# A fused attention and two-FFN kernel: the last matrix of batches 0 and 1 by half products, block sums in place, and a planner with other costs

## The chip, the cores and the metric

The kernel runs on one core of a Trainium2 chip. The metric is the device time of one execution in microseconds, from the first to the last instruction and what lies around them. The time before is the median of three runs.

## The reference

Shapes: q, k, v are (4 batches, 12 heads, 448 positions, 64), so there are 4 x 448 = 1792 tokens of width 768.

```python
scores = q @ k.T / sqrt(64)
scores = cap * tanh(scores / cap)            # cap = 30
attn = softmax(scores)                       # exp, then divided by sum + 1e-9
x = (attn @ v), heads side by side           # 1792 x 768
h = x @ w_in                                 # 768 x 2048
g = where(h >= 1, h, where(h <= -1, 0, (h + 1)**2 / 4))
y = g @ w_out                                # 2048 x 768
m = maximum(maximum(y @ w1, y @ w2), y @ w3) # each 768 x 768
out = m @ w_out2                             # 768 x 768, "the last matrix"
```

The weights arrive as 64-bit floats and are turned into 32-bit ones on the chip.

## The kernel before, in words

Everything is kept transposed: a tile holds 128 features by 448 positions of one batch (two batches side by side in a tile of the pool "u", 35 slots). Precision comes from splitting: a number is held as a rounded high part and the rest, and one **part**, 128 features times a 128 x 448 block, is three matmuls (high x high, high x low, low x high; lines 899 to 901 and 1117). Splitting costs one copy (`copy`, lines 310 and 312, on ScalarE or VectorE) and one subtraction (`tt`, line 315, VectorE).

The order of work is made by `Plan` (line 23). The kernel's functions register steps with `op(cost, fn, want, deps, uses, takes)`: a cost in microseconds for each engine that may do the step (A is ScalarE, D VectorE, T TensorE, Q the DMA queue of SyncE, P GpSimd, S a mere delay without an instruction), the wished time `want`, the steps it depends on and the buffers it takes. `Plan.run` plays the program through with these costs and gives each step to the engine that would end it first; buffers of a pool are handed out in order of `want`. `emit` then writes the instructions in that order, and on the chip each engine works through its own list in order, waiting on semaphores.

In order of time the work is:

- `attention(b, i, ...)` for batch b and pair of heads i (6 pairs): scores, tanh, exp, the sum over keys, the product with v, the division. The sums are made by adding the four key blocks of exp on VectorE (`add` in `attention`, line 717) and then one or more products with ones (`total4`, line 702, `SUM` each). `ADDED = (3, 2, 2, 3)` is the number of additions for each batch: 3 leave one tile for TensorE to sum, 2 leave two tiles. The row of sums is spread over partitions by GpSimd's and SyncE's DMAs (lines 788, 791, 796) around a reciprocal (line 809), and the delays S stand for those DMAs.
- `ffn(0)` for batch 0 while attention of batch 1 runs, then `ffn(1)` while attention of batches 2 and 3 runs. 16 blocks of w_in, 24 blocks of w_out. For batch 0 the weights come as 64-bit words and are made 32-bit in four steps (`fetch_first`, lines 412 to 441), then stored to scratch. The first `PLAIN = 6` blocks of w_in in batch 0 aren't split: `parts` multiplies them by one 32-bit matmul (line 894) with the unsplit `xf`.
- From then on pairs of batches go together, by **half products** (`strassen`, line 1018): a matrix is cut into 2 x 2 blocks and the two batches are the two columns of the other side, and seven products of halves (`STAGES`, line 1016) take the place of eight, at the price of additions. The inputs' sums and their splits (`divide`, t1 to t4, lines 1048 to 1090) fill 7 x K2 tiles named op of pool "u", each held until the last group of outputs has used it; a `lander` (line 1350) adds up the seven results of a group in VectorE and ScalarE. `first_two_end` does this for batches 0 and 1 with the three maximum matrices (layer 2, 9 groups of one block pair), and then takes the last matrix whole: M is split into 12 halves m, and for each of 6 blocks of the weights and each batch 6 parts are summed (lines 1454 to 1482). `last_two` does all four layers for batches 2 and 3 by half products.
- The weight blocks' sums for half products are made by `combine` (line 516: four loads into four wf buffers, four sums into one or two raw buffers), used by `store_sums` and `old_blocks` for batches 2 and 3, and by `new_blocks` (line 1169: sums in two raw buffers) for batches 0 and 1. Pools: raw 3, wf 5, w 4 slots.

Of the kernel before, what the change touches and what calls it, by code (L numbers as in the profile page):

```python
# [22 lines left out]
class Plan:  # L23
# [3 lines left out]

    LATENCY = 0.08  # L30
    AHEAD = 25.0
    TURN = 0.1
    STAY = 5.0
# [39 lines left out]
    def run(self):  # L73
# [42 lines left out]
        while left:  # L116
            moved = True
            while moved:
                moved = False
                ts = [o for o in ready if o.kind and at[id(o)] <= t + 1e-9 and can_take(o)]  # L120
                turn = min(ts, key=first) if ts else None

                only = dict.fromkeys(free_at, 0.0)
                for o in ready:
                    if len(o.cost) == 1 and at[id(o)] <= t + 1e-9:
                        e = next(iter(o.cost))
                        only[e] += o.cost[e]
                for o in ready:
                    if at[id(o)] > t + 1e-9 or o.kind and o is not turn:
                        continue  # L130
                    idle = [e for e in o.cost if free_at[e] <= t + 1e-9]
                    if not idle:
                        continue
                    e = next(iter(o.cost))
                    if len(o.cost) > 1:
                        ends = {e: max(free_at[e], t) + only[e] + c for e, c in o.cost.items()}
                        e = min(ends, key=ends.get)
                    if e not in idle or not can_take(o):
                        continue
# [24 lines left out]
                    left -= 1  # L164
                    moved = True
                    break
# [5 lines left out]
            while events and events[0][0] <= t + 1e-9:  # L172
# [7 lines left out]
                for x in o.out:  # L180
                    x.n -= 1
                    if not x.n:
                        r = max(
                            d.t1 + (0.0 if d.e in x.cost and len(x.cost) == 1 else self.LATENCY)
                            for d in x.deps
                        )
                        if "Q" in x.cost and x.takes:
                            r = max(r, x.want - self.AHEAD)
                        at[id(x)] = r
                        ready.append(x)  # L190
                        serial += 1
                        heapq.heappush(events, (r, serial, None))
# [52 lines left out]
def softcap_attention_two_ffn(  # L245
# [19 lines left out]
    D = 64  # L265
# [55 lines left out]
    def c_tt(n):  # L321
        return {"D": 1.03 * n + 0.155}
# [192 lines left out]
    halves = {}  # L515
    def combine(layer, m, run, want):

        n = RUN[layer]  # L520
        bufs, gots = {}, {}
        for i, j in ((1, 0), (1, 1), (0, 0), (0, 1)):
            u, o = corner(layer, m, i, j, run)
            wf = buf("wf", "wf", [P, WU])

            def load(e, u=u, o=o, wf=wf):
                nc.sync.dma_start(out=wf.tile[:, :n], in_=scratch[u][:, o : o + n])

            bufs[i, j] = wf
            gots[i, j] = op({"Q": 1.7 * n / 1000}, load, want - 8, [stored[u]], takes=[wf])  # L530
        wide = n * 4 * 4 > WU * 8
        ss = [buf("raw", "ss", [P, 2 if wide else 4, n]) for _ in range(2 if wide else 1)]
        c, d = ss[0], ss[-1]

        def s(x):
            return ss[x // 2].tile[:, x % 2] if wide else c.tile[:, x]

        def add(x, y, z, o, deps, uses, takes):
            def get(v):
                return bufs[v].tile[:, :n] if isinstance(v, tuple) else s(v)  # L540

            return op(
                c_tt(n / 1000), lambda e: tt(e, get(x), get(y), get(z), o), want, deps,
                [*uses, *takes], takes,
            )

        s1 = add(0, (1, 0), (1, 1), ALU.add, [gots[1, 0], gots[1, 1]],
                 [bufs[1, 0], bufs[1, 1]], [c])
        s2 = add(1, 0, (0, 0), ALU.subtract, [s1, gots[0, 0]], [bufs[0, 0], c], [])
        s3 = add(2, (0, 0), (1, 0), ALU.subtract, [gots[0, 0], gots[1, 0], s1],  # L550
                 [bufs[0, 0], bufs[1, 0], d], [d] if wide else [])
        s4 = add(3, (0, 1), 1, ALU.subtract, [s2, s3, gots[0, 1]], [bufs[0, 1], c, d], [])
        return s, ss, (s1, s2, s3, s4)

    def store_sums(layer, m, run, want):
        n = RUN[layer]
# [10 lines left out]
    def attention(b, i, begin, last):  # L567
# [207 lines left out]
        if small:  # L775
# [37 lines left out]
            recips.append(  # L813
                op({"Q": 0.7}, spread2, w + 0.3, [r], [rs], [rs] if pooled else [])
            )
        for k in range(0 if small else NCH):
            sl_ = slice(k * C, (k + 1) * C)
            recips.append(op(
# [350 lines left out]
    def new_blocks(layer, group, starts):  # L1169
# [17 lines left out]
            for i in range(2) for j in range(2)  # L1187
        }
        (u1, wf1, g1), (u2, wf2, g2) = wfs
        ss = [buf("raw", "ss", [P, 2 * n]) for _ in range(2)]  # L1190

        def part(x, y):
            return lambda: ss[x].tile[:, y * n : (y + 1) * n]

        s2, s3, s1, s4 = part(0, 0), part(0, 1), part(1, 0), part(1, 1)
        w = starts[2] - 11
# [4 lines left out]
                [*uses, *takes], takes,  # L1201
            )

        o1 = add(s1, a[1, 0], a[1, 1], ALU.add, [g2], [wf2], [ss[1]])
        o2 = add(s2, s1, a[0, 0], ALU.subtract, [o1, g1], [wf1, ss[1]], [ss[0]])
        o3 = add(s3, a[0, 0], a[1, 0], ALU.subtract, [g1, g2, o2], [wf1, wf2, ss[0]])
        o4 = add(s4, a[0, 1], s2, ALU.subtract, [o2, g1], [wf1, *ss])

        def both(get, n, srcs, deps, w):
# [8 lines left out]
            )  # L1218
            return wt, [hi, lo]

        def whole(b_):
            return lambda: b_.tile[:, : 2 * n]

        wa, da = both(whole(wf1), 2 * n, [wf1], [g1], starts[0] - 8)
        keep_divided(u1, wa, da, starts[0])
        wb, db = both(whole(ss[0]), 2 * n, [ss[0]], [o2, o3], starts[2] - 7)
        wc, dc = both(whole(ss[1]), 2 * n, [ss[1]], [o1, o4], starts[4] - 7)
# [211 lines left out]
    def first_two_end(base):  # L1439
# [15 lines left out]
        for j in range(2):  # L1455
            for m in range(NM):
                ms[m][j] = split(
                    "m", lambda m=m, j=j: M[m].tile[:, j], M[m], [mdone[m][j]], base - 4 + 0.1 * m
                )
        for m in range(NM):  # L1460
            u = W2 + m
            wf, got = fetch_again(u, base)
            w = divided(u, wf, got, base)
            if m < H2:
                keep_divided(u, *w, base)
            else:
                keep_divided(u, *w, base, KH)
            for j in range(2):
                ps, g = buf("m", "ps_m", [P, 512]), Group(NP)
                done = parts(  # L1470
                    0, lambda q: base + q * PART, (*w, False), [x[j] for x in ms], 0, NP, ps, g,
                    True,
                )
                for o in done[1:]:
                    o.deps.append(done[0])
                base += NP * PART
                o = half("o")
                c = op(
                    {"A": 0.53, "D": 0.62}, lambda e, o=o, ps=ps: copy(e, o.tile, ps.tile[:, :S]),
                    base, done, [ps], [o],  # L1480
                )
                send(lambda o=o: o.tile, o, m, j, [c], base + 0.6)
        return base

    def last_two(base):
# [127 lines left out]
```

## Time and profile before

| what | value |
| --- | --- |
| median of 3 runs | 955.91 us (955.85 to 959.21) |
| the profiled execution | 959.17 us |
| its span | 957.4 us |
| mean granted TensorE clock | 0.996 of full |
| busy: PE, PEld, DVE, ACT | 98%, 79%, 81%, 62% |
| chain that ended last | PE 90%, DMA 3%, DVE 3%, issue 2%, ACT 1% |

PE is TensorE's matmuls, PEld its weight loads, DVE VectorE, ACT ScalarE, POOL GpSimd, SP SyncE. The windows give the busy time of each engine in a stretch, with instructions in brackets, and then the granted clock, the mean busy share of the DMA engines and GB/s. Busy time counts overlapping instructions once. The chain of waits goes back from the last instruction to what released it each time.

### The profile page before, as it was taken

What the parts mean: (1) busy time and instruction counts of PE and PEld (TensorE: products, weight loads), DVE (VectorE), ACT (ScalarE), POOL (GpSimd) and SP (SyncE); (2) the same over time, 40 slices, a digit from 0 to 9 for tenths busy, and PEclk for the clock granted to TensorE, in tenths of its full rate; (3) what the DMA queues carried; (4) which work ended last, traced back from release to release, by engine and by line L of the source; (5) the groups of instructions that cost most, each with busy time, mean ns of one, the idle gap of its engine ahead of it and who ended that gap; (6) DMA issues with size and microseconds to landing.
All of it is one profiled execution on the core that took longest, in us unless ns stands there. A gap on an engine that the chain in (4) does not pass through costs nothing.

```text
span 957.4 us, 14768 instructions
## 1 busy us (share of the span) xinstructions
PE 937.2 (98%) x5323; PEld 755.6 (79%) x5323; DVE 778.0 (81%) x1288; ACT 594.5 (62%) x932; POOL 14.7 (2%) x27
## 2 busy tenths in 40 slices
PE   7789999999999999999999999999999999999997
PEld 1134788777767676678999999999999999899997
DVE  2898898897989888888888848887889869758782
ACT  7968888775888877774434316566865715233441
POOL 0000000000000000000000000000000000000000
PEclk9989999999999999999999999999999999999999
DMA  7758768998888998853777887442233345446343
GB/s 201 220 154 267 236 191 245 274 287 270 291 280 279 302 292 259 232 173 118 253 265 271 288 295 255 123 140 80 90 101 109 111 121 184 144 147 205 108 148 120
DMA packets 95339, 194.48 MB, mean 203 GB/s; under 512 B 12094, under 2 KB 56858, under 8 KB 95258
## 3 DMA queue, kind: packets, MB, share of 16 engines
q1 hardware_dynamic: 94378, 193.36, 64.0%
q8 instruction: 44, 0.72, 0.3%
q0 software_dynamic: 736, 0.10, 0.1%
q14 instruction: 37, 0.30, 0.1%
q10 hardware_dynamic: 144, 0.00, 0.0%
HBM read 142.51 MB, written 50.81 MB: 202 GB/s over the span
## 4 chain that ended last, share of the span: by engine, by line
PE 90%; DMA 3%; DVE 3%; issue 2%; ACT 1%; SPq 0%; POOL 0%; DVEq 0%; ACTq 0%; POOLq 0%
PE ps_m L1117 32%; PE ps_s L1117 11%; PE ps_m L899 9%; PE ps_m L901 8%; PE ps_m L900 8%; PE ps_a L836 6%; PE ps_s L615 5%; PE ps_a L1117 5%; PE ps_m L894 3%; PE ps_r L709 1%; DMA qk<-in_qk 1%; DMA rc<-rs 1%; DVE op L315 1%; DVE se L315 1%; PE ps_s L626 1%
## 5 line engine op out<-in xcount | busy, mean ns | idle before, releaser
L1117 PE MATMUL ps_m<-op,w 128*128 128x448 f32 x1575 | 324.0, 365 | 0.6 <-DVE M L315 0.6
L1117 PEld LDWEIGHTS ps_m<-op,w 128*128 128x128 f32 x1575 | 295.7, 188 | 24.4 <-DVE M L315 1.0
L315 DVE TENSOR_TENSOR w<-wf,w 128x512 fp32r<-128x512 f32 (+2 forms) x155 | 117.6, 761 | 13.8 <-ACT w L310 11.4
L310 ACT ACTIVATE w<-wf 128x512 fp32r<-128x512 f32 (+2 forms) x120 | 81.1, 679 | 70.4 <-PE ps_m L1117 30.9
L633 ACT ACTIVATE t<-ps_s,qscale 112x896 f32<-112x896 f32 x96 | 93.4, 1004 | 33.0 <-PE ps_s L615 25.2
L1117 PE MATMUL ps_s<-op,w 128*128 128x448 f32 x522 | 110.7, 366 | 0.4 <-DVE op L315 0.2
L1117 PEld LDWEIGHTS ps_s<-op,w 128*128 128x128 f32 x522 | 98.0, 188 | 8.7 <-ACT op L310 0.5
L680 ACT ACTIVATE t<-t,cap_sb 112x896 f32<-112x896 f32 x96 | 95.9, 1038 | 0.3
L310 ACT ACTIVATE w<-ss 128x384 fp32r<-128x384 f32 (+1 forms) x93 | 53.1, 583 | 64.9 <-PE ps_m L1117 37.5
L836 PE MATMUL ps_a<-t,v 112*32 112x448 f32 (+1 forms) x752 | 79.4, 543 | 5.2 <-ACT t L680 2.7
L899 PE MATMUL ps_m<-g,w 128*128 128x448 f32 x192 | 72.6, 378 | 0.0
L315 DVE TENSOR_TENSOR w<-ss,w 128x384 fp32r<-128x384 f32 (+1 forms) x98 | 59.8, 627 | 14.3 <-ACT w L310 14.0
L901 PE MATMUL ps_m<-g,w 128*128 128x448 f32 x192 | 70.3, 366 | 0.0
L900 PE MATMUL ps_m<-g,w 128*128 128x448 f32 x192 | 70.3, 366 | 0.0
L836 PEld LDWEIGHTS ps_a<-t,v 112*32 112x32 f32 (+1 forms) x752 | 22.2, 110 | 51.3 <-issue 33.1
L899 PE MATMUL ps_m<-x,w 128*128 128x448 f32 x156 | 58.7, 376 | 0.0
L423 DVE SCALAR_TENSOR_TENSOR raw<-raw 128x768 int32<-128x768 int32 (+1 forms) x64 | 55.4, 867 | 3.0 <-ACT raw L412 2.5
L900 PE MATMUL ps_m<-x,w 128*128 128x448 f32 x156 | 57.1, 366 | 0.6 <-DVE x L315 0.6
L439 DVE SCALAR_TENSOR_TENSOR wf<-raw 128x768 int32<-128x768 int32 (+1 forms) x64 | 54.7, 856 | 3.1 <-ACT raw L431 1.6
L901 PE MATMUL ps_m<-x,w 128*128 128x448 f32 x156 | 57.0, 366 | 0.0
L1117 PE MATMUL ps_a<-op,w 128*128 128x448 f32 x234 | 51.3, 365 | 0.0
L1117 PEld LDWEIGHTS ps_a<-op,w 128*128 128x128 f32 x234 | 44.0, 188 | 3.5
(142 smaller groups left out, 1424.8 us busy)
## 6 DMA issues: line engine op xcount, KB each, us to landing
wf<-w SPq DMA_DIRECT2D x104, 192.0 KB
wf<-w SPq DMA_DIRECT2D x66, 256.0 KB
w<-wf SPq DMA_DIRECT2D x40, 384.0 KB
wf<-w SPq DMA_DIRECT2D x40, 384.0 KB
raw<-in_w SPq DMA_DIRECT2D x18, 768.0 KB
w<-p SPq DMA_DIRECT2D x36, 384.0 KB
raw<-in_w_in SPq DMA_DIRECT2D x16, 768.0 KB
raw<-in_w_out SPq DMA_DIRECT2D x24, 512.0 KB
```

The source lines that it names most:

```text
L310: nc.scalar.activation(out=out_, in_=in_, func=AF.Copy)
L315: nc.vector.tensor_tensor(out=out_, in0=a, in1=b, op=o)
L423: nc.vector.scalar_tensor_tensor(out=lo, in0=hi, scalar=-(2**31), in1=lo, op0=ALU.bitwise_and, op1=ALU.bitwise_or,)
L439: nc.vector.scalar_tensor_tensor(out=wf.tile[:, :n].bitcast(I32), in0=hi, scalar=3, in1=lo, op0=ALU.logical_shift_left, op1=ALU.bitwise_or,)
L615: nc.tensor.matmul(ps.tile[:C, j, :S], k.tile[o, 1, c * C : (c + 1) * C], q.tile[o, 0], start=n == 0, stop=n == 2,)
L633: nc.scalar.activation(out=t[c].tile, in_=ps.tile[:C, :, :S], func=AF.Tanh, scale=qscale[:C])
L680: lambda e, c=c: nc.scalar.activation(out=t[c].tile, in_=t[c].tile, func=AF.Exp, scale=cap_sb[:C]),
L836: nc.tensor.matmul(pa.tile[j * D + d : j * D + d + n, :S], vt.tile[:, j, c, d : d + n], t[c].tile[:, j], start=start, stop=stop,)
L899: nc.tensor.matmul(ps.tile[:, :S], wh, a.tile[:, 0], start=start, stop=False)
L900: nc.tensor.matmul(ps.tile[:, :S], wh, a.tile[:, 1], start=False, stop=False)
L901: nc.tensor.matmul(ps.tile[:, :S], wl, a.tile[:, 0], start=False, stop=stop)
L1117: nc.tensor.matmul(get(), w_, x_, start=start and z == 0, stop=stop and z == 2, skip_group_check=begun,)
```

## The change

Six edits in one: `first_two_end` hands the last matrix to `strassen` as `last_two` does; `PLAIN` becomes 0; `ADDED` becomes 3 for batches 1 and 2 too; `combine` loads its four blocks by one step into one raw buffer (with a wf buffer for w_out's wider blocks), neighbours in one DMA, and adds in place; `new_blocks` puts its four sums in one raw buffer; the planner's numbers change. Of the last: `LATENCY` 0.09, a `LAP` by which A and D are free again before a step's end, the latency now also between two steps of A or D that follow each other, a delay of 5.0 for batch 0's gather of sums (3.0 before), and a delay of 2.0 behind the spreading DMAs.

```diff
-    LATENCY = 0.08
+    LATENCY = 0.09
+    LAP = {"A": 0.1, "D": 0.08}
...
-                        free_at[e] = t + c
+                        free_at[e] = t + c - self.LAP.get(e, 0.0)
...
-                            d.t1 + (0.0 if d.e in x.cost and len(x.cost) == 1 else self.LATENCY)
+                            d.t1 + (0.0 if d.e == "T" and "T" in x.cost else self.LATENCY)
...
-    PLAIN = 6
+    PLAIN = 0
...
-    ADDED, FOURS, POOLED = (3, 2, 2, 3), (0, 1, 2, 3), ()
+    ADDED, FOURS, POOLED = (3, 3, 3, 3), (0, 1, 2, 3), ()
...
     def combine(layer, m, run, want):
         n = RUN[layer]
-        for i, j in ((1, 0), (1, 1), (0, 0), (0, 1)):
-            u, o = corner(layer, m, i, j, run)
-            wf = buf("wf", "wf", [P, WU])
...
-            gots[i, j] = op({"Q": 1.7 * n / 1000}, load, want - 8, [stored[u]], takes=[wf])
+        fit = 4 * n <= WU * 2
+        raw = buf("raw", "ss", [P, 2 * WU])
+        wf = None if fit else buf("wf", "wf", [P, WU])
...
+                if fit and u == u1 and o1 == o + n:
+                    y = 2 * (1 - i) * n
+                    nc.sync.dma_start(
+                        out=raw.tile[:, y : y + 2 * n], in_=scratch[u][:, o : o + 2 * n]
+                    )
+                    continue
...
+        s1 = add((1, 1), (1, 0), (1, 1), ALU.add, [got])
+        s3 = add((1, 0), (0, 0), (1, 0), ALU.subtract, [s1])
+        s2 = add((0, 0), (1, 1), (0, 0), ALU.subtract, [s1, s3])
+        s4 = add((0, 1), (0, 1), (0, 0), ALU.subtract, [s2])
...
-            r = op({"S": 3.0 if first else 5.0}, lambda e: None, w + 0.06, [r], [rc, src])
+            r = op({"S": 5.0}, lambda e: None, w + 0.06, [r], [rc, src])
...
+            r = op({"Q": 0.7}, spread2, w + 0.3, [r], [rs], [rs] if pooled else [])
+            recips.append(op({"S": 2.0}, lambda e: None, w + 0.3, [r], [rs]))
...
-        ss = [buf("raw", "ss", [P, 2 * n]) for _ in range(2)]
+        ss = [buf("raw", "ss", [P, 2 * WU])]
...
     def first_two_end(base):
...
-        ms = [[None] * 2 for _ in range(NM)]
...
-        for m in range(NM):
-            u = W2 + m
-            wf, got = fetch_again(u, base)
-            w = divided(u, wf, got, base)
...
+        O = [unit(f"O01_{m}") for m in range(NM)]
+
+        def land_o(m, g, i):
+            def finish(i, j, o, w):
+                f = m + H2 * i
+                send(lambda: O[f].tile[:, j], O[f], f, j, [o], w)
+
+            return lander(O[m], O[m + H2], 1, finish)
+
+        base = strassen(
+            3, base, True, list(zip(M, mdone)), [[x] for x in range(N2[3])], land_o, new_blocks,
+            two_banks,
+        )
         return base
```

## Rows read from the trace of the kernel before

**Rows 1.** The page: busy time and instructions of each engine
```profile
PE 937.2 (98%) x5323; PEld 755.6 (79%) x5323; DVE 778.0 (81%) x1288; ACT 594.5 (62%) x932; POOL 14.7 (2%) x27
```
**Rows 2.** Windows (engines PE, PEld, DVE, ACT, POOL): start, two slices with idle PE, end
```profile
0.00:63.50 63.50, 50.63 (x424) 13.28 (x424) 41.59 (x62) 49.55 (x54) 3.36 (x9) 0.96 0.68 192
...
240.00:264.00 24.00, 22.87 (x166) 16.62 (x164) 21.70 (x33) 20.51 (x29) 0.61 (x1) 1.00 0.90 296
...
792.00:816.00 24.00, 23.65 (x116) 21.33 (x115) 21.59 (x42) 15.06 (x31) 0.00 (x0) 1.00 0.53 164
...
952.00:957.40 5.40, 0.23 (x2) 0.00 (x0) 0.00 (x0) 0.55 (x1) 0.00 (x0) 0.93 0.24 84
```
**Rows 3.** Windows: the two FFN stretches, the last matrix and its neighbours, the fullest window
```profile
63.50:216.00 152.50, 152.50 (x875) 112.08 (x874) 135.47 (x211) 126.92 (x190) 3.02 (x5) 0.99 0.81 247
...
216.00:432.00 216.00, 214.87 (x1466) 151.34 (x1468) 185.15 (x275) 171.51 (x224) 8.34 (x13) 1.00 0.83 262
...
447.00:631.00 184.00, 183.36 (x906) 169.91 (x906) 150.41 (x257) 79.08 (x139) 0.00 (x0) 1.00 0.69 234
...
549.00:593.00 44.00, 44.00 (x219) 40.77 (x218) 28.84 (x49) 15.27 (x31) 0.00 (x0) 1.00 0.79 281
...
593.00:631.00 38.00, 38.00 (x190) 35.20 (x189) 32.29 (x63) 24.58 (x48) 0.00 (x0) 1.00 0.42 127
...
120.00:144.00 24.00, 24.00 (x152) 19.97 (x152) 22.49 (x35) 21.52 (x31) 0.00 (x0) 1.00 0.61 192
```
**Rows 4.** Chain of waits: plain products and one pair's sums; start us, us, what
```profile
69.29 22.00 PE ps_m L894 x58
...
115.25 0.90 PE ps_r L709 x16
```
**Rows 5.** Timeline of PE, two L899 three matmuls apart in a split layer
```profile
425.71 0.37 PE L899 MATMUL ps_m<-g,w 128*128 128x448 f32 x1
...
426.33 0.37 PE L899 MATMUL ps_m<-g,w 128*128 128x448 f32 x1
```
**Rows 6.** Chain of waits: the long run of half products
```profile
447.65 102.41 PE ps_m L1117 x504
```
**Rows 7.** Groups by line and shape: costs of one instruction (mean ns)
```profile
L315 DVE TENSOR_TENSOR w<-wf,w 128x768 fp32r<-128x768 f32 x50 | 47.6, 953 | 1.5 <-ACT w L310 1.2
...
L310 ACT ACTIVATE w<-wf 128x768 fp32r<-128x768 f32 x35 | 29.4, 840 | 15.2 <-PE ps_m L1117 9.6 <-PE ps_m L901 3.8 <-ACT M L310 0.9
...
L315 DVE TENSOR_TENSOR se<-se,t 112x896 f32<-112x896 f32 x24 | 26.0, 1084 | 2.7 <-ACT t L680 1.5
...
L315 DVE TENSOR_TENSOR op<-M,op 128x448 fp32r<-128x448 f32 x18 | 10.6, 619 | 0.4 <-ACT op L310 0.3
...
L310 ACT ACTIVATE op<-M 128x448 fp32r<-128x448 f32 x16 | 8.9, 573 | 17.6 <-DVE M L315 17.6
...
L315 DVE TENSOR_TENSOR ss<-wf 128x384 f32<-128x384 f32 x58 | 32.0, 551 | 0.0
```
**Rows 8.** Timeline of DVE: neighbours in one queue; start us, us
```profile
582.47 0.62 DVE L315 TENSOR_TENSOR t<-X,X 128x448 f32<-128x448 f32 x1
...
583.01 0.62 DVE L315 TENSOR_TENSOR op<-X,op 128x448 fp32r<-128x448 f32 x1
```
**Rows 9.** Windows: DVE copies of L312 alone in that stretch
```profile
447.00:631.00 184.00, 8.27 (x17) 1.00 0.69 234
```
**Rows 10.** Timelines of PE and DVE, and the clock (windows), where the first layer begins
```profile
46.69 2.46 PE L836 MATMUL ps_a<-t,v 112*32 112x448 f32 x24 [2.49 <-DVE xf L315]
...
63.56 4.33 PE L894 MATMUL ps_m<-xf,wf 128*128 128x448 f32 x8
...
68.72 0.64 DVE L315 TENSOR_TENSOR xf<-ps_a,rs 128x448 f32<-128x448 f32 x1
...
72.98 0.63 DVE L315 TENSOR_TENSOR x<-xf,x 128x448 fp32r<-128x448 f32 x1 [1.68 <-ACT x L310]
...
62.00:66.00 4.00, 4.00 (x14) 2.17 (x11) 3.90 (x7) 3.59 (x5) 0.00 (x0) 0.54 0.18 60
```

More of the change, by code (lines that the diff above doesn't have):

```diff
@@ L520, in combine @@
         n = RUN[layer]
-        bufs, gots = {}, {}
-        for i, j in ((1, 0), (1, 1), (0, 0), (0, 1)):
-            u, o = corner(layer, m, i, j, run)
-            wf = buf("wf", "wf", [P, WU])
-            def load(e, u=u, o=o, wf=wf):
-                nc.sync.dma_start(out=wf.tile[:, :n], in_=scratch[u][:, o : o + n])
-            bufs[i, j] = wf
-            gots[i, j] = op({"Q": 1.7 * n / 1000}, load, want - 8, [stored[u]], takes=[wf])
-        wide = n * 4 * 4 > WU * 8
-        ss = [buf("raw", "ss", [P, 2 if wide else 4, n]) for _ in range(2 if wide else 1)]
@@ L533, in combine @@
[L533 to L540, printed above, removed]
+        fit = 4 * n <= WU * 2
+        raw = buf("raw", "ss", [P, 2 * WU])
+        wf = None if fit else buf("wf", "wf", [P, WU])
+        bufs = [raw] if fit else [raw, wf]
+        at = {}
+        for y, (i, j) in enumerate(((1, 0), (1, 1), (0, 0), (0, 1))):
+            if fit or y < 3:
+                at[i, j] = lambda y=y: raw.tile[:, y * n : (y + 1) * n]
+            else:
+                at[i, j] = lambda: wf.tile[:, :n]
@@ new lines, in combine, with load @@
+        where = {q: corner(layer, m, *q, run) for q in at}
+        def load(e):
+            for i in (1, 0):
+                (u, o), (u1, o1) = where[i, 0], where[i, 1]
+                if fit and u == u1 and o1 == o + n:
[4 more added lines that the diff above has]
+                    continue
+                for j in range(2):
+                    u, o = where[i, j]
+                    nc.sync.dma_start(out=at[i, j](), in_=scratch[u][:, o : o + n])
@@ L542, in add @@
+        got = op(
+            {"Q": 1.7 * 4 * n / 1000}, load, want - 8, [stored[u] for u, _ in where.values()],
+            takes=bufs,
+        )
+        def add(out, x, y, o, deps):
             return op(
-                c_tt(n / 1000), lambda e: tt(e, get(x), get(y), get(z), o), want, deps,
-                [*uses, *takes], takes,
-            )
-        s1 = add(0, (1, 0), (1, 1), ALU.add, [gots[1, 0], gots[1, 1]],
-                 [bufs[1, 0], bufs[1, 1]], [c])
-        s2 = add(1, 0, (0, 0), ALU.subtract, [s1, gots[0, 0]], [bufs[0, 0], c], [])
@@ L550, in combine @@
[L550 to L553, printed above, removed]
+                c_tt(n / 1000), lambda e: tt(e, at[out](), at[x](), at[y](), o), want, deps, bufs
+            )
+        s1 = add((1, 1), (1, 0), (1, 1), ALU.add, [got])
+        s3 = add((1, 0), (0, 0), (1, 0), ALU.subtract, [s1])
@@ L555, in store_sums @@
+        s2 = add((0, 0), (1, 1), (0, 0), ALU.subtract, [s1, s3])
+        s4 = add((0, 1), (0, 1), (0, 0), ALU.subtract, [s2])
+        sums = [at[q] for q in ((1, 1), (0, 0), (1, 0), (0, 1))]
+        return lambda x: sums[x](), bufs, (s1, s2, s3, s4)
     def store_sums(layer, m, run, want):
@@ L812, in attention @@
             r = op({"Q": 0.1}, spread, w + 0.2, [r], [rc])
-            recips.append(
-                op({"Q": 0.7}, spread2, w + 0.3, [r], [rs], [rs] if pooled else [])
-            )
+            r = op({"Q": 0.7}, spread2, w + 0.3, [r], [rs], [rs] if pooled else [])
+            recips.append(op({"S": 2.0}, lambda e: None, w + 0.3, [r], [rs]))
         for k in range(0 if small else NCH):
@@ L1189, in new_blocks @@
         (u1, wf1, g1), (u2, wf2, g2) = wfs
-        ss = [buf("raw", "ss", [P, 2 * n]) for _ in range(2)]
+        ss = [buf("raw", "ss", [P, 2 * WU])]
         def part(x, y):
-            return lambda: ss[x].tile[:, y * n : (y + 1) * n]
+            return lambda: ss[0].tile[:, (2 * x + y) * n : (2 * x + y + 1) * n]
         s2, s3, s1, s4 = part(0, 0), part(0, 1), part(1, 0), part(1, 1)
@@ L1202, in add @@
             )
-        o1 = add(s1, a[1, 0], a[1, 1], ALU.add, [g2], [wf2], [ss[1]])
-        o2 = add(s2, s1, a[0, 0], ALU.subtract, [o1, g1], [wf1, ss[1]], [ss[0]])
-        o3 = add(s3, a[0, 0], a[1, 0], ALU.subtract, [g1, g2, o2], [wf1, wf2, ss[0]])
+        o1 = add(s1, a[1, 0], a[1, 1], ALU.add, [g2], [wf2], ss)
+        o2 = add(s2, s1, a[0, 0], ALU.subtract, [o1, g1], [wf1, *ss])
+        o3 = add(s3, a[0, 0], a[1, 0], ALU.subtract, [g1, g2, o2], [wf1, wf2, *ss])
         o4 = add(s4, a[0, 1], s2, ALU.subtract, [o2, g1], [wf1, *ss])
@@ L1219, in both, with whole @@
             return wt, [hi, lo]
-        def whole(b_):
-            return lambda: b_.tile[:, : 2 * n]
+        def whole(b_, o=0):
+            return lambda: b_.tile[:, o : o + 2 * n]
         wa, da = both(whole(wf1), 2 * n, [wf1], [g1], starts[0] - 8)
         keep_divided(u1, wa, da, starts[0])
-        wb, db = both(whole(ss[0]), 2 * n, [ss[0]], [o2, o3], starts[2] - 7)
-        wc, dc = both(whole(ss[1]), 2 * n, [ss[1]], [o1, o4], starts[4] - 7)
+        wb, db = both(whole(ss[0]), 2 * n, ss, [o2, o3], starts[2] - 7)
+        wc, dc = both(whole(ss[0], 2 * n), 2 * n, ss, [o1, o4], starts[4] - 7)
         wd = buf("w", "w", [P, 2, WU], F32R)
@@ L1453, in first_two_end @@
         )
-        ms = [[None] * 2 for _ in range(NM)]
-        for j in range(2):
-            for m in range(NM):
[L1457 to L1460, printed above, removed]
-            u = W2 + m
-            wf, got = fetch_again(u, base)
-            w = divided(u, wf, got, base)
[L1464 to L1482, printed above, removed]
+        O = [unit(f"O01_{m}") for m in range(NM)]
[7 more added lines that the diff above has]
+            two_banks,
+        )
         return base
```

## The prediction, made before the changed kernel was run

> **What bounds the kernel now.** I read the page's engine shares first: matmuls fill 98% of the span [rows 1]. The windows then say where the other 20.2 us (957.4 less 937.2) lie: 12.9 before 63.5 us, 5.2 behind the last matmul, and the 2 left in three slices between, of which the first and the last stand there [rows 2]. So from the first FFN layer on a matmul taken out shortens the run, unless another engine becomes the limit. How near one is, is read stretch by stretch [rows 3]. In the first FFN (63.5 to 216) VectorE is busy for 89% and ScalarE for 83%; in the second (216 to 432) 86% and 79%; around the last matrix (447 to 631) 82% and 43%. The fullest slice has VectorE at 93.7% and both together at 91.7%; I take these as the most that the static order gets out of them.
>
> **What leaves TensorE.** Three things, all of them instructions that are gone.
> - Split first blocks: 6 blocks x 6 parts = 36 parts. A plain part leaves two records, so 58 records in 22.00 us are 0.759 us a part [rows 4]; a split part in the FFN takes 0.62 us, from one L899 to the next but one group [rows 5]. 36 x 0.139 = 5.0 us.
> - One sum per pair in batches 1 and 2: 12 times one product with ones less. Two took 0.90 us [rows 4], so 12 x 0.45 = 5.4 us, 2.7 in each FFN.
> - The last matrix: 72 parts become 3 groups x 7 stages x 3 = 63. At 102.41/504 x 3 = 0.610 us a part [rows 6], 9 are 5.5 us.
>
> Together 15.9 us. That is the gain if the matmuls stay gapless.
>
> **What VectorE and ScalarE get instead.** An instruction holds VectorE less long than it lasts: one of 0.62 us at 582.47 is followed at 583.01 [rows 8], that is 0.54, 0.08 less. By the same difference 768 columns (0.953) hold it for 0.87 and 384 (0.551) for 0.47 [rows 7].
>
> First FFN. Six splits: 6 x 0.87 = 5.2 on VectorE, 6 copies at 0.84 less the same 0.08 [rows 7] (an estimate for ScalarE), 4.5 there. Six additions over keys at 1.08 [rows 7], 6.5; the third addition hangs on the second, so I take nothing off. 262.4 us of work on both becomes 278.6. TensorE wants 152.5 - 7.7 = 144.8 us, which would need 96.2% of both. At the fullest slice's 91.7% the stretch takes 151.9. So of 7.7 us between 0.6 and 7.7 comes; no row lies nearer to one end, and I take the middle, 4. The second FFN gets six additions: 363.2 of 2 x 213.3 us is 85%, below the limit, so they are hidden beside matmuls and the 2.7 counts in full. Without that cover they would cost 6.5.
>
> The last matrix. Counted in subtractions and additions on VectorE: t1 to t4, 4 x 3 = 12; splits of inputs 21 where there were 12, 9 more; the lander's sums 4 x 3 = 12; each of these at 0.54, the rows' nearest shape [rows 7, 8]: 17.8. The weights: four sums for each of 3 groups, 12 x 0.47 = 5.6; their splits 9 x 0.87 + 3 x 0.47 where there were 6 x 0.87: 4.0. In all 27.5 us more. From 447 to 631 VectorE had 150.4 busy [rows 3]; it would have 177.9 in 184 - 5.5 = 178.5 us. That can't be met. What can leave it are its copies, 8.3 us [rows 9], which the planner may give to ScalarE, busy for 79 of 184. Then 169.6 at 93.7% is 181.0 us, a gain of 3.0. If none moves, 177.9 at 93.7% is 189.9, a loss of 5.9. If in addition nothing of it can be done before 549, the 61.1 us of [rows 3] from 549 to 631 become 88.6, at 93.7% 94.6 us in place of 82: a loss of 12.6. The other end is the matmuls' 5.5. I take a gain of 2, near the case with the copies moved, since ScalarE is the emptiest engine there.
>
> One wait is new at the border. With the columns swapped, stage A11 needs M2 of batch 1, the last result of the matrix before. From that product to the operand lie a maximum, a copy and a subtraction, some 1.8 us by 0.62, 0.57 and 0.62 [rows 7], and two parts (1.2 us) stand in front; 0.6 us at most is TensorE's, and what queues behind it on VectorE are t1 and t2 of the same block. It lies inside the 2 that I take.
>
> **The planner and the buffers.** The new numbers issue nothing; they change who stands where in each list. VectorE's deduction of 0.08 fits the spacing in [rows 8], and a delay for the spreading DMA is nearer to the chip than none: TensorE waited 2.49 us for an xf behind those DMAs [rows 10]. After 63.5 us such gains are bounded by the 2 us of idle TensorE. Before it they are bounded by that wait and the slow clock: the granted clock was 0.54 of 2.4 GHz from 62 to 66 us, mostly the lower level, where 8 records took 4.33 us, against 3.0 at the pace of [rows 4]. Against them stands the split: plain parts began with xf, the last of which started at 68.72, while a split one needs the x that started at 72.98 [rows 10], 4.3 us later. Between plus 3.8 and minus 4.3 I take 0.
>
> The sums in place are as many instructions as before. On SyncE's queue 20 of the 26 combinations load by two DMAs instead of four; the last matrix loads, stores and keeps as many blocks as before, and GpSimd's gathers stay. The combined load waits for a raw buffer, where it needed only wf; behind it on the queue stand other weight loads. TensorE asks for the sums two stages after the group's start, 11 us with groups of three, so I count nothing; without that cover a late set of sums would cost four of them, 1.9 us.
>
> **The sum.** 4 + 2.7 + 2 + 0 = 8.7 us. The profiled execution took 959.17 us, 3.3 more than the median of 955.91; 959.2 - 8.7 = 950.5, and against the median 947.2. That is the forecast.
>
> **Rivals.**
> - TensorE stays gapless. For it: the planner now knows of the room that [rows 8] shows. Against it: 96% of both engines in the first FFN. It gives 955.9 - 15.9 = 940.0, with the start's 3.8 as well 936.2.
> - VectorE and ScalarE are the bound in the first FFN, and the last matrix returns nothing: 0.6 + 2.7 + 0 = 3.3 us, 952.6. For it: the windows of [rows 3]. Against it: a planner that spreads work over neighbouring stretches.
> - Slower: the input tiles op block the pool. The matrix before holds 21 of 35 slots until its last group, and M takes six; so the last matrix can hardly prepare before 549, and the 12.6 us above are paid, less 3.3 from the FFNs: 965.2. It decides when the added work that can't start before 549 is more than the idle VectorE there, 82 - 61.1 = 21 us. For it: VectorE idles from 549 to 593 (28.8 of 44) and not before. Against it: eight slots are free even then, each stage of the last group gives back three, and weights don't need that pool.
> - VectorE runs its instructions one at a time, each for its whole length. Then the added work is 17.2 us in the first FFN and 31.6 at the last matrix; with the copies moved 173.7 at 93.7% is 185.4, and the gains are 0.1 + 2.7 - 1.4: 954.5. The starts of [rows 8] speak against it. The Trainium skill (VectorE: DVE Perf Modes, The DRAIN you can't avoid) says that the next operation starts only once the pipe of the one before is empty, and elsewhere in that section that one which isn't held starts earlier; these rows show the second.
>
> **Chances.** The forecast 0.52, with a range of its own from 943 to 951; gapless matmuls 0.18; the second rival 0.16; whole lengths 0.03; the pool 0.11. A measurement can tell 0.5% here, so faster is below 951.1 us and slower above 960.7. Faster 0.52 + 0.18 = 0.70; same 0.16 + 0.03 = 0.19; slower 0.11. The range goes from 938 to 957: it takes in the forecast, the second and fourth rival with some room for a late start, and the gapless case without all of the start's gain; the pool's 0.11 and the low end of the gapless case are left out, some 0.17.
>
> **What would show it.** In the chain of waits L894 must be gone and L1117 must begin where L899 on m stood. Right would be: 63 parts in about 40 to 42 us at the last matrix, with VectorE's share from 447 to 631 above 90% and fewer copies on it; a first FFN some 4 us shorter with both engines near 94%; a second one shorter by 2 to 3 us with no new wait. Wrong would be: matmuls of L1117 waiting for op or w by several microseconds behind 549 (the pool or VectorE), a first FFN as long as before (the second rival), a granted clock below full after 70 us, or a gain that lies before 63.5 us, where I put nothing.

## The result and the profile after

The changed kernel took 949.5 us in the median of five runs (947.54 to 951.08), the kernel before 958.63 in five: a ratio of 0.9903, 95% interval 0.9873 to 0.9932. That is 9.1 us less; 8.7 were forecast. The two profiled executions took 959.17 and 951.08 us, 8.1 apart, and the stretches below are of these two.

The engine shares from the page of the changed kernel, to be read beside [rows 1]: 87 matmul records fewer, VectorE 38 us fuller, ScalarE 11 us emptier.

```profile
PE 926.8 (98%) x5236; PEld 755.3 (80%) x5236; DVE 816.3 (86%) x1385; ACT 583.4 (61%) x922; POOL 14.5 (2%) x27
```

The windows of both kernels, cut where the work changes instead of at the fixed times of [rows 3]: up to the first product of the FFN, up to batch 0's last product with w_out, up to the first half product, up to the last matrix of batches 0 and 1, up to the end of that, the rest. First the kernel before.

```profile
0.00:63.56 63.56, 50.69 (x424) 13.28 (x425) 41.65 (x62) 49.61 (x54) 3.36 (x9) 0.96 0.68 192
63.56:227.87 164.31, 164.31 (x961) 120.68 (x960) 144.31 (x224) 130.95 (x195) 3.62 (x6) 0.99 0.80 248
227.87:434.08 206.21, 205.08 (x1394) 143.68 (x1393) 177.34 (x264) 167.54 (x218) 7.73 (x12) 1.00 0.83 260
434.08:549.90 115.82, 115.18 (x568) 106.34 (x567) 102.20 (x169) 46.06 (x74) 0.00 (x0) 1.00 0.72 246
549.90:593.67 43.77, 43.77 (x217) 40.56 (x216) 28.61 (x50) 15.57 (x30) 0.00 (x0) 1.00 0.78 275
593.67:957.40 363.73, 358.20 (x1765) 331.04 (x1763) 283.87 (x523) 184.81 (x362) 0.00 (x0) 1.00 0.42 130
```

And the changed kernel:

```profile
0.00:63.12 63.12, 52.91 (x437) 15.23 (x437) 43.23 (x63) 54.25 (x62) 3.36 (x9) 0.95 0.76 212
63.12:222.27 159.15, 156.36 (x937) 125.28 (x936) 148.69 (x233) 131.63 (x197) 3.63 (x6) 0.99 0.82 253
222.27:422.30 200.03, 199.39 (x1314) 141.30 (x1313) 182.90 (x274) 158.03 (x209) 7.56 (x12) 1.00 0.86 263
422.30:543.00 120.70, 120.62 (x601) 107.30 (x600) 109.78 (x188) 48.20 (x82) 0.00 (x0) 1.00 0.71 243
543.00:584.00 41.00, 39.19 (x191) 35.20 (x190) 40.78 (x74) 24.07 (x46) 0.00 (x0) 1.00 0.90 318
584.00:949.30 365.30, 358.32 (x1765) 331.02 (x1763) 290.90 (x559) 167.25 (x329) 0.00 (x0) 1.00 0.39 125
```

The first column after the times is the stretch's length. The start is 0.4 us shorter, the first FFN 5.2, the second 6.2, the last matrix 2.8. The maximum matrices (fourth line) are 4.9 us longer, and the rest 1.6. Of the first FFN's 5.2 some 1.4 are matmuls of scores (12 records) that now stand before the FFN; so the FFN gained 3.8, and the start, with more to do, 1.8. Of the second FFN's 6.2 some 3.1 are a pair's product with v (32 records) that now stands behind the first half product, not ahead of it; so the FFN gained 3.1, and the maximum matrices lost 1.8. In the fifth line VectorE is busy for 40.78 of 41.00 us.

In the first FFN TensorE is now idle for 2.8 us, where it was never idle before. Right behind, from 70 to 74 us, the granted clock was 0.57 of full, mostly the lower level; a matmul began 0.37 us after the one before, where 0.20 is the pace at full clock:

```profile
66.00:70.00 4.00, 1.80 (x8) 1.35 (x9) 4.00 (x7) 4.00 (x6) 0.00 (x0) 1.00 0.35 41
70.00:74.00 4.00, 4.00 (x14) 3.56 (x13) 4.00 (x6) 2.77 (x5) 0.00 (x0) 0.57 0.79 285
```

The waits of TensorE in the changed kernel, longest first (us in total, times, longest):

```profile
PE ps_s L633 <- DMA qk<-in_qk: 4.3, 1, 4.3
PE ps_s L622 <- ACT t L640: 2.2, 2, 1.9
PE ps_m L905 <- DVE xf L316: 2.1, 1, 2.1
PE ps_m L1123 <- ACT O L311: 1.4, 1, 1.4
...
PE ps_m L1123 <- DVE O L316: 0.4, 1, 0.4
```

The first was there before. The third lies in the first FFN: a split needs x, which is made from xf, where a plain product began with xf itself. The last two shown are new and both lie at the border to the last matrix. A timeline of the changed kernel around them (start, duration, engine, line, [idle before, what ended it]):

```profile
546.27 0.67 PE L1123 MATMUL ps_m<-op,w 128*128 128x448 f32 x2
...
547.03 0.84 ACT L311 ACTIVATE w<-wf 128x768 fp32r<-128x768 f32 x1 [1.67 <-PE ps_m L1123]
...
547.78 0.53 ACT L311 ACTIVATE O<-ps_m 128x448 f32<-128x448 f32 x1
...
548.36 2.27 PE L1123 MATMUL ps_m<-op,w 128*128 128x448 f32 x9 [1.42 <-ACT O L311]
...
550.36 0.61 DVE L316 TENSOR_TENSOR O<-ps_m,O 128x448 f32<-128x448 f32 x1
...
551.02 0.67 PE L1123 MATMUL ps_m<-op,w 128*128 128x448 f32 x2 [0.39 <-DVE O L316]
```

O is where the results are collected. A stage writes its product into a bank, and the third stage takes the bank of the first, which must be copied out before. That copy (O) stands behind a copy of weights in ScalarE's list, and TensorE waits for 1.42 us; the next bank waits for a sum on a VectorE that hasn't paused for several microseconds.

### The profile page after: what moved, and what is told of

It is laid out like the page before. It is cut to its first block, busy times and chain, and to the rows that moved or that the text cites. A ratio compares the mean times of both kernels' runs of the same rounds, so it can differ in the third digit from the quotient of the medians.

```text
span 949.3 us, 14557 instructions
## 1 busy us (share of the span) xinstructions
PE 926.8 (98%) x5236; PEld 755.3 (80%) x5236; DVE 816.3 (86%) x1385; ACT 583.4 (61%) x922; POOL 14.5 (2%) x27
## 4 chain that ended last, share of the span: by engine, by line
PE 89%; DVE 5%; ACT 4%; issue 1%; DMA 0%; DVEq 0%; ACTq 0%
PE ps_m L1123 35%; PE ps_s L1123 11%; PE ps_m L905 9%; PE ps_m L907 8%; PE ps_m L906 8%; PE ps_a L842 7%; PE ps_a L1123 5%; PE ps_s L622 5%; ACT t L640 2%; ACT t L687 1%; PE ps_r L716 1%; DVE se L316 1%; DVE w L316 1%; DVE op L316 1%; DVE M L316 1%
## 5 line engine op out<-in xcount | busy, mean ns | idle before, releaser
L1123 PE MATMUL ps_m<-op,w 128*128 128x448 f32 x1764 | 365.3, 367 | 1.8 <-ACT O L311 1.4
L1123 PEld LDWEIGHTS ps_m<-op,w 128*128 128x128 f32 x1764 | 330.8, 188 | 32.6 <-ACT O L311 1.8
L316 DVE TENSOR_TENSOR w<-wf,w 128x512 fp32r<-128x512 f32 (+2 forms) x161 | 121.3, 756 | 4.4 <-ACT w L311 3.7
L311 ACT ACTIVATE w<-wf 128x512 fp32r<-128x512 f32 (+2 forms) x113 | 77.5, 688 | 76.0 <-PE ps_m L1123 26.3
L311 ACT ACTIVATE w<-ss 128x384 fp32r<-128x384 f32 (+1 forms) x83 | 48.7, 595 | 66.0 <-PE ps_m L1123 47.9
L842 PE MATMUL ps_a<-t,v 112*32 112x448 f32 (+1 forms) x752 | 81.4, 557 | 1.5 <-ACT t L687 0.9
L905 PE MATMUL ps_m<-x,w 128*128 128x448 f32 x192 | 73.0, 380 | 2.1 <-DVE xf L316 2.1
L316 DVE TENSOR_TENSOR w<-ss,w 128x384 fp32r<-128x384 f32 (+1 forms) x104 | 65.6, 643 | 7.6 <-ACT w L311 7.0
L906 PE MATMUL ps_m<-x,w 128*128 128x448 f32 x192 | 71.0, 370 | 0.7 <-DVE x L316 0.7
L907 PE MATMUL ps_m<-x,w 128*128 128x448 f32 x192 | 70.9, 369 | 0.0
L316 DVE TENSOR_TENSOR ss<-ss 128x384 f32<-128x384 f32 (+1 forms) x98 | 54.7, 574 | 0.3
L316 DVE TENSOR_TENSOR se<-se,t 112x896 f32<-112x896 f32 x48 | 51.9, 1080 | 2.8 <-ACT t L687 2.2
```

The source lines that it names most:

```text
L311: nc.scalar.activation(out=out_, in_=in_, func=AF.Copy)
L316: nc.vector.tensor_tensor(out=out_, in0=a, in1=b, op=o)
L842: nc.tensor.matmul(pa.tile[j * D + d : j * D + d + n, :S], vt.tile[:, j, c, d : d + n], t[c].tile[:, j], start=start, stop=stop,)
L905: nc.tensor.matmul(ps.tile[:, :S], wh, a.tile[:, 0], start=start, stop=False)
L906: nc.tensor.matmul(ps.tile[:, :S], wh, a.tile[:, 1], start=False, stop=False)
L907: nc.tensor.matmul(ps.tile[:, :S], wl, a.tile[:, 0], start=False, stop=stop)
```

## Experiments

Each kernel was timed on the same chip beside runs of the kernel before. The ratio is to those; that of the changed kernel, run again, was 0.9906.

**The same kernel again.**

> The changed kernel once more, unchanged, for a second trace of the same program. Theory A (the distance between two matmuls of a half-product layer, 0.2067 us in the first layer of batches 0 and 1 and 0.2027 elsewhere, is set by how the run happens to be phased): the stretches with 0.2067 us lie elsewhere or are missing, and the time moves by up to 2 or 3 us with them. Rival B (it is set by the program, its tiles or its waits): the same layers have 0.2067 us again. Time by both: 947 to 952 us, 0.990 of the kernel before.

948.01 us, 0.9906 (0.9878 to 0.9934). With the same program, this profiled execution reaches the first FFN after 59.9 us where the other took 63.1, and its matmuls are busy for 5.2 us less:

```profile
PE 921.6 (98%) x5236; PEld 754.4 (80%) x5236; DVE 816.2 (86%) x1385; ACT 583.8 (62%) x922; POOL 14.5 (2%) x27
```

So two executions of one program can differ by that much, and the stretches of a single one are no finer than this where they hold the start or the spacing of matmuls.

The chain of waits shows that spacing, the distance from one matmul's start to the next. For the changed kernel, the run of half products in the maximum matrices, the one that begins in the last matrix, at 551 us, and one in the last layer (start, us, what, records):

```profile
431.34 93.21 PE ps_m L1123 x450
...
551.02 38.57 PE ps_m L1123 x189
...
925.59 5.58 PE ps_m L1123 x27
```

93.21/450 is 0.2071 us for the first, 38.57/189 is 0.2041 from 551 us on, 5.58/27 is 0.2067 near the end; the kernel before had 0.2032 [rows 6]. Windows of 48 us count it: the changed kernel has 234 records in the maximum matrices, 238 later, and 118 in 24 us near its end:

```profile
456.00:504.00 48.00, 48.00 (x234) 43.60 (x233) 42.53 (x72) 17.51 (x28) 0.00 (x0) 1.00 0.75 258
600.00:648.00 48.00, 48.00 (x238) 44.48 (x237) 37.42 (x74) 26.04 (x50) 0.00 (x0) 1.00 0.31 102
912.00:936.00 24.00, 24.00 (x118) 21.80 (x117) 12.06 (x25) 6.22 (x13) 0.00 (x0) 1.00 0.34 117
```

The same program again, and the same layers:

```profile
456.00:504.00 48.00, 48.00 (x234) 43.58 (x234) 42.70 (x72) 18.21 (x30) 0.00 (x0) 1.00 0.69 239
...
908.00:932.00 24.00, 24.00 (x120) 22.24 (x120) 12.21 (x25) 6.37 (x13) 0.00 (x0) 1.00 0.34 117
```

The maximum matrices have the long distance both times, the last layer only once. So neither A nor B holds alone: the distance takes one of two values and keeps it for long stretches, and for the last layer the program doesn't fix which.

**The planner's numbers alone, and all but them.** On the kernel before, and undone in the changed one:

```diff
-    LATENCY = 0.08
+    LATENCY = 0.09
+    LAP = {"A": 0.1, "D": 0.08}
...
-                            d.t1 + (0.0 if d.e in x.cost and len(x.cost) == 1 else self.LATENCY)
+                            d.t1 + (0.0 if d.e == "T" and "T" in x.cost else self.LATENCY)
...
-            r = op({"S": 3.0 if first else 5.0}, lambda e: None, w + 0.06, [r], [rc, src])
+            r = op({"S": 5.0}, lambda e: None, w + 0.06, [r], [rc, src])
```

> The kernel before with the planner's new numbers alone (latency, lap, the two delays); no instruction is added or removed. Theory (the gain is matmuls taken out; the numbers only reorder): within 3 us of the kernel before, since TensorE idled for 12.9 us before 63.5 us and 2 us after it. Rival (the new order carries the gain, the matmuls were hidden anyway): 947 to 951 us, 0.990 to 0.993 of before.

954.07 us, 0.9959 (0.9929 to 0.9990): 4 us of gain from the order alone, between the two expectations.

> The changed kernel with the planner's old numbers; every instruction stays. Theory: within 3 us of the changed kernel, 0.988 to 0.994 of before, unless the old numbers, which charge VectorE 0.08 us too much for each instruction, make the order of the fuller VectorE worse; then up to 5 us slower than the changed kernel. Rival (the order carries the gain): the time of the kernel before, ratio 0.997 or more.

958.57 us, 1.0020 (0.9997 to 1.0043). With 87 records fewer and the old numbers, the kernel is no faster than before. Its page and its waits of TensorE:

```profile
PE 927.0 (97%) x5236; PEld 754.9 (79%) x5236; DVE 811.4 (85%) x1328; ACT 623.5 (65%) x979; POOL 14.8 (2%) x27
```

```profile
PE ps_r L715 <- DVE se L315: 10.5, 6, 4.0
```

The work is the same; but ScalarE does 57 instructions more than in the changed kernel and VectorE 57 fewer, and TensorE waits 10.5 us for the additions over keys (se), 7.7 of it in the first FFN.

**Which of the numbers.** Three kernels, each the changed one with one part of the new numbers taken back: the lap, the delays, or the latency with its rule.

```diff
-    LAP = {"A": 0.1, "D": 0.08}
+    LAP = {}
```

> The changed kernel without the planner's lap; latency and delays stay new. Theory C (the planner must know that VectorE's and ScalarE's instructions overlap by 0.08 to 0.1 us, or else it spreads their work too thin and TensorE waits for the third addition): 5 to 9 us slower than the changed kernel, about the time before, with waits of the product with ones for se. Rival D (the delays of the DMAs do it): within 2 us of the changed kernel.

953.06 us, 0.9934 (0.9906 to 0.9961), by the ratios 3 us more than the changed kernel, with intervals that overlap: between theory C and rival D. ScalarE has 979 instructions again.

```diff
-            r = op({"S": 5.0}, lambda e: None, w + 0.06, [r], [rc, src])
+            r = op({"S": 3.0 if first else 5.0}, lambda e: None, w + 0.06, [r], [rc, src])
...
-            recips.append(op({"S": 2.0}, lambda e: None, w + 0.3, [r], [rs]))
+            recips.append(r)
```

> The changed kernel with the old delays (3.0 for batch 0's gather, none behind the spreading DMA); lap and latency stay new. Theory C: within 2 us of the changed kernel in the FFNs; what is lost lies before 63.5 us, where TensorE waits for xf, 1 to 4 us. Rival D: 5 us or more slower, with waits behind 63.5 us.

948.67 us, 0.9896 (0.9861 to 0.9932): as the changed kernel. But the waits for se are back:

```profile
PE ps_r L716 <- DVE se L316: 8.7, 6, 2.7
```

```diff
-    LATENCY = 0.09
+    LATENCY = 0.08
...
-                            d.t1 + (0.0 if d.e == "T" and "T" in x.cost else self.LATENCY)
+                            d.t1 + (0.0 if d.e in x.cost and len(x.cost) == 1 else self.LATENCY)
```

> The changed kernel with the old latency and its old rule (none between two steps of one engine); lap and delays stay new. Of the 10 us that the old numbers cost in all, the lap alone gave 3 and the delays none. Theory E (this rule holds the rest, since a chain of three additions on VectorE looks shorter to the planner than it is): 4 to 8 us slower than the changed kernel, with TensorE's products with ones waiting for se. Rival F (none of the numbers holds the rest alone; lap and rule together do, one covers for the other): within 3 us of the changed kernel.

947.66 us, 0.9878 (0.9846 to 0.9909): not slower, so theory E fails by its time. By the total only the lap costs something when it alone is missing. The first FFN of the four kernels says more; in order all old numbers, no lap, old delays, old rule:

```profile
63.72:231.20 167.48, 159.42 (x950) 125.37 (x948) 151.01 (x230) 141.00 (x208) 3.64 (x6) 0.98 0.78 246
59.99:223.31 163.32, 156.70 (x936) 124.79 (x936) 149.65 (x229) 134.50 (x202) 3.62 (x6) 0.99 0.82 254
60.31:221.70 161.39, 155.79 (x943) 124.48 (x942) 153.73 (x240) 133.03 (x196) 3.62 (x6) 1.00 0.83 261
58.26:220.98 162.72, 156.41 (x935) 125.35 (x936) 155.47 (x243) 129.63 (x193) 3.90 (x6) 0.99 0.83 258
```

TensorE idles there for 8.1, 6.6, 5.6 and 6.3 us; in the changed kernel it was 2.8 both times. So in these traces each part of the new numbers keeps some 3 to 4 us of waits away. In the last two kernels the total doesn't show them. Part of what makes up for them is the end: 5.2 us behind the last matmul, where the changed kernel has 7.0 and 6.9; but the kernel without the lap has 5.2 as well. The rest is not told apart from the spacing of matmuls.

**The parts, one by one.** The last matrix by whole products again (`first_two_end` as before):

```diff
-        base = strassen(
-            3, base, True, list(zip(M, mdone)), [[x] for x in range(N2[3])], land_o, new_blocks,
...
+            w = divided(u, wf, got, base)
```

> The changed kernel with the last matrix of batches 0 and 1 by whole products again, 72 parts for 63. Theory (of its 5.5 us, 2.8 came through, as the two profiles say): 2 to 4 us slower than the changed kernel, 0.993 to 0.994 of before. Rival 1 (VectorE's 27 us more hold up the neighbours, so that the step costs more than it brings): the same time or faster than the changed kernel. Rival 2 (all of it comes through): 5.5 us slower, 0.996 of before.

951.41 us, 0.9942 (0.9913 to 0.9971): 3.4 us more, as the theory has it, though the intervals overlap. Its profiled execution took 959.83 us, 8.4 over the median. It has 234 records in 48 us, the long distance, in every layer from the maximum matrices on:

```profile
600.00:648.00 48.00, 48.00 (x234) 43.60 (x233) 36.23 (x70) 25.71 (x50) 0.00 (x0) 1.00 0.27 91
800.00:848.00 48.00, 48.00 (x234) 43.58 (x233) 36.51 (x72) 15.85 (x33) 0.00 (x0) 1.00 0.37 123
```

The first six blocks unsplit:

```diff
-    PLAIN = 0
+    PLAIN = 6
```

> The changed kernel with the first six blocks of batch 0 unsplit again (PLAIN = 6). TensorE gets 5.0 us more, VectorE and ScalarE 9.7 us less. Theory (with the new numbers the first FFN takes up nearly all that is freed: the stretch to batch 0's last block product got 5.2 us shorter, of 7.7): 2 to 4 us slower than the changed kernel, 0.993 to 0.995 of before. Rival (first FFN bound by VectorE and ScalarE): within 1 us of the changed kernel.

950.49 us, 0.9903 (0.9871 to 0.9935), within what can't be told from the changed kernel. The first FFN's window is longer by 4.2 us all the same; first this kernel, then the changed one's second run:

```profile
58.90:222.00 163.10, 160.85 (x907) 117.69 (x906) 153.45 (x244) 122.38 (x181) 4.35 (x6) 1.00 0.80 255
```

```profile
59.87:218.76 158.89, 156.10 (x937) 125.24 (x936) 148.97 (x233) 131.99 (x197) 3.63 (x6) 0.99 0.80 254
```

It starts 1.0 us earlier, so 3.2 are left at the FFN's end. These two executions take 946.58 and 946.46 us: this kernel gets back 2.4 in the maximum matrices (118.3 us against 120.7) and 1.8 behind the last matmul (5.2 against 6.9). So the splits shorten their stretch by some 3 of 5.0 us in these traces, and the total doesn't show it.

Two sums per pair again in batches 1 and 2:

```diff
-    ADDED, FOURS, POOLED = (3, 3, 3, 3), (0, 1, 2, 3), ()
+    ADDED, FOURS, POOLED = (3, 2, 2, 3), (0, 1, 2, 3), ()
```

> The changed kernel with two sums per pair in batches 1 and 2 again: TensorE 5.4 us more, VectorE 13 us less. Theory: 3 to 5.5 us slower than the changed kernel, 0.994 to 0.996 of before. Rival (the third addition is what VectorE can't afford; with the old numbers TensorE waited 10.5 us for it): within 1 us, or faster.

951.81 us, 0.9930 (0.9901 to 0.9958): 2.3 us more than the changed kernel by the ratios, a little under the theory's range, with intervals that overlap. One sum alone takes 0.52 us in the changed kernel, where two took 0.90 [rows 4], so one less is worth 0.38 and not 0.45:

```profile
91.35 0.52 PE ps_r L716 x8
```

The weight blocks' sums as before (`combine` and `new_blocks` whole):

```diff
-        raw = buf("raw", "ss", [P, 2 * WU])
...
+            wf = buf("wf", "wf", [P, WU])
...
+        ss = [buf("raw", "ss", [P, 2 if wide else 4, n]) for _ in range(2 if wide else 1)]
```

> The changed kernel with the weight blocks' sums as before: four wf buffers and one or two raw buffers for each set, four loads, two raw buffers for batches 0 and 1. Theory (sums in place are as many instructions; they free buffers, which nothing waited for): within 1.5 us of the changed kernel. Rival (the buffers let VectorE prepare earlier, which the fuller VectorE around the last matrix needs): 2 us or more slower, with longer waits of the half products for w.

951.6 us, 0.9924 (0.9894 to 0.9955), 1.7 us more by the ratios; the intervals overlap. In its profile TensorE waits 2.8 us at the border to the last matrix, not 1.4, and that matrix takes 43.0 us for 41.0. This speaks for the rival, without settling it: the longer wait is for the copy out of a bank, and the half products wait for w by only 0.6 us.

**The border.**

```diff
-            return lander(O[m], O[m + H2], 1, finish)
+            return lander(O[m], O[m + H2], 0, finish)
...
-            3, base, True, list(zip(M, mdone)), [[x] for x in range(N2[3])], land_o, new_blocks,
+            3, base, False, list(zip(M, mdone)), [[x] for x in range(N2[3])], land_o, new_blocks,
```

> The changed kernel, where the last matrix of batches 0 and 1 takes its columns unswapped, so that its first stage reads batch 0's maxima, which end earlier than batch 1's. Theory (the 2.6 us that the 63 parts take over their 38.4 are VectorE full from 524 to 555 us, the border's order matters little): the last matrix takes 40 to 42 us as now, the time moves by less than 1.5 us. Rival (the late operand of the first stage holds it up): 38.5 to 39.5 us, 1.5 to 2.5 us faster.

946.04 us, 0.9885 (0.9844 to 0.9926). The window of the last matrix:

```profile
539.74:578.78 39.04, 38.57 (x191) 35.42 (x190) 38.97 (x70) 23.98 (x45) 0.00 (x0) 1.00 0.94 334
```

39.04 us where 41.00 stood in both runs of the changed kernel, and VectorE just as full. The total can't tell 2 us, by its interval; the window can, and it is 38.9 in the next kernel. So the theory is wrong: it wasn't the fullness of VectorE that cost the 2 us. The rival's time is right, but it doesn't come about as the rival says: in neither kernel does a matmul there wait for the late operand itself. What changes with it is the order of the lists. ScalarE's in this kernel has

```profile
541.81 0.55 ACT L311 ACTIVATE O<-ps_m 128x448 f32<-128x448 f32 x1 [0.66 <-PE ps_m L1123]
...
543.63 0.85 ACT L311 ACTIVATE w<-wf 128x768 fp32r<-128x768 f32 x1 [0.34 <-PE ps_m L1123]
```

The first copy out of a bank comes 2.1 us after the matrix's start and stands ahead of the copy of weights; in the changed kernel it comes after 4.8 us, behind that copy.

**The lap alone, with the border mended.** Both edits above together with the old delays and the old rule.

> The changed kernel with the lap as the only one of the planner's new numbers (old latency and rule, old delays) and with the columns of the last matrix of batches 0 and 1 unswapped. Theory G (the lap alone carries what the new numbers give, and the unswapped columns save 2 us at the last matrix): 942 to 946 us, 0.983 to 0.988 of before, the 63 parts in 39 to 39.5 us. Rival (the lap needs the rule or the delays beside it, each could be missing only while the others were there): 948 to 956 us, with TensorE waiting for se by 5 us or more in the first FFN; the last matrix in 39 to 39.5 us all the same.

946.5 us, 0.9875 (0.9853 to 0.9897), the last matrix in 38.9 us. The time falls just above G's range and its ratio inside; but TensorE waits for se, 4.2 us of it in the first FFN, a little less than the rival has it:

```profile
PE ps_r L716 <- DVE se L316: 6.6, 6, 2.1
```

So the lap is enough for the total, and the waits don't go with it. This kernel and the one with the border mended alone beat the kernel before; against the changed kernel both are lower by 2 to 3 us by the ratios, with intervals that overlap.

## Why the prediction held, and where its steps were wrong

**The first FFN**: 4 forecast, 5.2 measured, of 7.7; 3.8 without the scores that moved ahead of it. The limit I put on both engines wasn't met: VectorE and ScalarE together were busy for 280.3 of 2 x 159.15 us, 88%, where I had reckoned with 94. The two hold only 5.1 us more work than before, not 16.2; they did 6.2 us more before the FFN began, where three of the weights' new splits and the tanh and exp behind those scores now stand. Most of what is missing of the 7.7 is not spread over the stretch, as that limit would have it, but lies at its beginning, in the 2.8 us of waits for xf and x. I had counted this wait with the start, at 4.3 us at most. VectorE doesn't pause there (4.00 of 4.00 us from 66 to 70): reciprocals and a weight stand ahead of the xf that TensorE waits for. The low clock from 70 to 74 us is a sign that I had named for being wrong; the kernel before had one of its own from 62 to 66 [rows 10].

**The second FFN**: 2.7 forecast, 3.1 measured. The additions were hidden as said; VectorE rose from 86 to 91%. At 0.38 us each the six sums are 2.3 of it, and 0.5 are waits that went.

**The last matrix**: 2 forecast, 2.8 in the profiles, 3.4 by undoing it. VectorE's added work was counted right: from the first half product to the end it has 441.5 us where it had 414.7, 26.8 more for 27.5. The step that failed is the ceiling of 93.7%: VectorE ran at 99.5% through the whole matrix. The fullest slice of a kernel that TensorE bounds shows what was asked of an engine, not what it can do. Of the copies, 8.3 us, some 6.1 stayed on it. The waits at the border are 1.8 us, not 0.6, and TensorE doesn't wait for the operand's own chain, as I had it, but for a copy out of a bank behind a copy of weights.

**The planner's numbers**: 0 forecast, and this step was wrong. I bounded them by TensorE's idle time in the kernel before, which says nothing of the idle time that the other edits would cause. The old numbers with all the edits give nothing (1.0020); the new ones alone give 4 us (1 to 7 by the interval). "They change who stands where in each list" also left out that they choose the engine of each copy; that this choice makes the waits isn't shown, since the kernels with the old delays and the old rule have 929 and 917 instructions on ScalarE, near the changed kernel's 922, and wait too. What the sum took for the edits' own gain is theirs only under the new numbers, and over those it is some 5 us (0.9959 to 0.9906) and not 8.7. So it is in part luck that 8.7 met 9.1: by the experiments some 4 of it come from a term put at nothing, and by the stretches a gain at the start made up for losses that I hadn't foreseen.

**The sums in place**: nothing forecast; undone, they cost some 2 us, which the runs don't settle.

**The rivals.** Gapless matmuls (15.9 us) didn't come. TensorE's busy time fell by 10.4 us in one run of the changed kernel and by 15.6 in the other, but 4.6 us of waits are new in the first FFN and the last matrix, and 1.8 behind the last matmul. The second comes nearest to what the old numbers make of the change, a first FFN no shorter than before with TensorE idle for 8.1 us of it; but the two other engines are busy for only 87% of it there, so it isn't that they are full. The pool didn't block: TensorE's waits at the last matrix are 1.8 us, and none is for op. VectorE's overlap of neighbouring instructions is there in the changed kernel too: 547.61 to 548.15 for one of 0.62 us.

**What was not foreseen** in the sum: a gain at the start, 1.8 us in these two executions, where I had put nothing; as two runs of one program differ there by 3.2, it isn't shown to be the change's. The maximum matrices are 1.8 us longer, by the longer distance of their matmuls (567 at 0.004 are 2.3), and 7.0 us lie behind the last matmul where there were 5.2. The last has no cause that I can show; it comes back in the second run of the same program (6.9) and, of the eleven other kernels, in only one (6.8).

## What to carry to other kernels

Taking work from the bounding engine is worth what the order lets the others absorb: give the planner the real spacing of instructions before counting on it, and test edits under the plan that goes with them. An engine's fullest slice in a run that another engine bounds is no ceiling. Where two layers meet, look at what stands ahead of the copies that free the banks. When a total doesn't move, compare the waits stretch by stretch: two parts of the planner's numbers each kept some 3 us of waits away in the traces, and undoing them left the total as it was.

## What the runs showed of the hardware

The distance between two matmuls of a half product, 128 x 128 by 448 columns, has two values at the full clock, some 0.2027 and 0.2067 us; it holds one for tens to hundreds of microseconds. In the changed kernel it was long up to the border of the last matrix (234 records in 48 us), short behind the pauses there (238) and long again near the end (5.58 us for 27). One kernel kept the longer for all of its half products and took 959.83 us in that execution, 8.4 over its median. Two runs of one program had it in the same place in one layer and in only one of them in another. What sets it was not tried.

VectorE can be kept busy at 99% for 40 us by a static list (40.78 of 41.00 us), with the next instruction starting 0.08 us before the last one ends.

In the changed kernel the granted clock was full from 63 to 70 us, a stretch in which TensorE waited for 0.66 and 2.13 us, and 0.57 from 70 to 74.
